# Two-token loads, ScalarE's first issues and an in-flight cast of half of w_out, in a fused RWKV attention and feed-forward kernel

## The chip, the cores and the metric

The kernel runs on 1 core of one Trainium2 chip. The metric is the device time of one execution in microseconds (us), the median of several runs. TensorE is PE in the profile (PEld is its weight load), VectorE is DVE, ScalarE is ACT, GpSimd is POOL, and SyncE, which issues most of the DMAs, is SP.

## The reference, cut to what matters

```python
# r, k, v: (4, 8, 768, 48) f32 (batch, head, token, dim); w, u: (8, 48); w_in: (384, 2048); w_out: (2048, 384)
for t in range(S):
    cur = np.einsum('bhd,bhe->bhde', u[None] * kt, vt)
    y[:, :, t] = np.einsum('bhd,bhde->bhe', rt, state + cur)
    state = w[None, :, :, None] * state + np.einsum('bhd,bhe->bhde', kt, vt)
x = y.transpose(0, 2, 1, 3).reshape(B * S, H * D)          # 3072 tokens x 384
h = x @ w_in
g = np.where(h >= 1, h, np.where(h <= -1, 0.0, (h + 1) ** 2 / 4))
out = g @ w_out
```

## The kernel before, in words

**Units.** The 4 x 768 tokens are cut into 24 units of 128 tokens (C = 128; unit i is batch i mod 4, chunk i div 4). Two units make a block m of 256 tokens (UB = 2, 12 blocks). The kernel has no loop at run time on its main path: everything is unrolled, and the data stay on the core between the stages.

**Attention of a unit** (`attention`, L469). K, R and V of the unit are loaded as 128 tokens by 8 heads by 48 (`add_load`, L417: tiles K, R, Vf; each row that the DMA moves is 48 floats, 192 bytes). K times `Winv` (w to the power -j-1, op "kw", L483) and R times `Wpow` (w to the power i, "rw", L487) go to one bf16 tile KR; PE or a DMA transposes it to RK ("tr" L505 and "rk", or "trd" L524). "at" (L535) forms K times R for all token pairs in two PSUM tiles, "mask" (L550, L553) keeps the lower triangle on DVE; "P", "dg", "dc" (L565, L571, L579) get the diagonal term with u on PE for units below `dmm`, and two GpSimd multiplications with a DVE sum (L585, L586, L591) for the others. "vd" (L596) multiplies the diagonal by V, "y" (L606, L609) is the product with V and with the carried state, "x" (L621) adds the two. "xp" and "xt" (L631) transpose x on PE for units below `xpe`; the others use a DMA transpose (L639). "x2" (L647) sums the squares of x for a bound. "st", "t", "tw", "bd" (L657, L664, L668, L672) carry the state. The first four units have no earlier state.

**The feed-forward** takes xT. `layer1` (L697): per block eight groups "L1" of six matmuls (L715) of 128 by 128 weights with 256 tokens, each group squared by ACT into g (L730; (h/2 + 1/2) squared, and a check at the end repeats the work in full only where some |h| could exceed 0.95). `layer2` (L735): per unit four groups "L2" of four matmuls (L749) with 384 columns, group s using quarter s of w_out; then a copy of the output tile and its store.

**The weights** w_in and w_out come in four quarters each, I0 to I3 and O0 to O3 (L443 to L462): a f32 load of 768 KB into a staging tile wf (5 slots), and three or four casts to bf16 by whichever of ACT, DVE and POOL the planner picks (profile line L318, the helper `copy`).

**The order.** `Plan.run` (L98) is a list scheduler run at build time. Each operation has a table of engines with costs, a due time (CFG "due", "step" and "bias"), buffers and dependences; it writes out one fixed order for each engine, and each engine then runs its list strictly in that order. The order of the first loads on SP comes from CFG "order": U0 to U3 (the loads of units 0 to 3), I0 to I3, O0, O1, O2, U4, U5, O3, U6, U7. All loads and stores are issued by SP, but for one small load of u by ACT (L379). Each DMA issued by SP or ACT takes one of eight completion semaphores in turn, so each one waits for the one eight before it.

**Fillers.** Until a planned time PE runs matmuls on a zero tile wherever it would otherwise be idle (L403, "wm"). They are placed in the fixed order too.

**Start.** w is loaded, spread to 128 partitions by two matmuls (L367), its logarithm lw is taken by ACT (L373), then `Winv` and `Wpow` by two exponentials (L375, L376).

Of the kernel before, what the change touches and what calls it, by code (L numbers as in the profile page):

```python
# [16 lines left out]
CFG = {  # L17
    "order": "U0 U1 U2 U3 I0 I1 I2 I3 O0 O1 O2 U4 U5 O3 U6 U7",
    "tpe": 10,
    "dmm": 8,  # L20
    "xpe": 6,
    "pair": 4,
    "cold": 9.0,
    "fine": 0,
    "am0": 2,
    "am1": 0,
    "norm": 100.0,
    "wide": 0,
    "due": [32.65, 38.55, 28.55, 31.54, 45.68],
    "step": 9.83,  # L30
    "warm": 24.0,
# [3 lines left out]
    "bias": {  # L35
        "P": 2.76, "am": -14.26, "at": -12.0, "bd": -7.97, "cI": 4.41, "cO": 11.29, "c_uw": 4.37, "dc": 5.73,
        "dg": 7.99, "ku": -5.64, "kw": 7.93, "ldK": -0.11, "ldR": 0.75, "ldVf": 1.96, "mask": -7.09, "red": 3.59,
        "rk": -1.31, "rkk": 0.04, "rkr": 5.61, "rw": -4.62, "st": 7.95, "t": -0.44, "tr": 0.61, "trd": -2.94,
        "trk": -6.22, "trr": 1.71, "tw": -8.79, "v": 0.76, "vd": -0.65, "x": 1.06, "x2": 1.39, "xp": -2.11,
        "xt": 0.98, "xtd": -1.36, "y": -5.96,  # L40
    },
# [20 lines left out]
class Plan:  # L62
# [35 lines left out]
    def run(self):  # L98
# [13 lines left out]
        while len(done) < len(todo):  # L112
# [47 lines left out]
            if e == "DVE" and o.sb and free["POOL"] > est + 0.15:  # L160
                occ, lat = occ + free["POOL"] - est - 0.15, lat + free["POOL"] - est - 0.15
            if e == "PE" and est < CFG["cold"] and o.name[:2] != "wm":
                occ, lat = 2.0 * occ, lat + occ
# [55 lines left out]
def kernel(  # L219
# [30 lines left out]
    while len(D_m) < NB + 2:  # L250
# [10 lines left out]
        "K": 6, "R": 6, "Vf": 6, "wf": 5, "KR": 4, "KU": 3, "V": 6, "RK": 4, "AT": 3, "P": 2, "VD": 3, "dg": 3,  # L261
        "x": 5, "x2": 2, "g": 5, "os": 3, "sq": 1, "ss": 2, "am": 2,
    }
    P = Plan(slots)
    rows = rot.tile([1, 2, H, DP], F32, name="rows", tag=f"g_{slots['g'] - 1}")
    lw = rot.tile([128, H, D], F32, name="lw", tag="x2_1")

    def get(b, shape, dtype):
        pl = psum if b.pool in ("a", "h", "o") else rot
        nm = f"{b.pool}_{b.slot}"  # L270
        b.t = pl.tile(shape, dtype, name=nm, tag=nm)
        return b.t
# [3 lines left out]

    nc.scalar.preload_act_table_set("natural_log_exp_and_others")

# [14 lines left out]
    i_col = const.tile([128, 1], F32, name="i_col")  # L293
    negj_col = const.tile([128, 1], F32, name="negj_col")
    Wpow = const.tile([128, H, D], F32, name="Wpow")
    Winv = const.tile([128, H, D], F32, name="Winv")
# [23 lines left out]
    def pair(t, p):  # L320
        return t[:, 2 * p : 2 * p + 2, :].rearrange("q h d -> q (h d)")
# [5 lines left out]
    heads = lambda t: t.rearrange("p (h d) -> p h d", h=H)  # L327
    c_wr = P.op("c_wr", {"SP": (0.5, 0)}, lambda e: nc.sync.dma_start(out=w_sp[0:128:64, :], in_=w.rearrange("(s h) d -> s (h d)", s=2)), due=-1000, dma=(0.05, 1, 0.5))
    c_ubc = P.op("c_ubc", {"SP": (0.4, 0)}, lambda e: nc.sync.dma_start(out=u_bc, in_=row_bcast(u)), due=D_m[CFG["dmm"] // UB] - 25, dma=(0.7, 8, 0.6))
    c_cols = P.op("c_col", {"POOL": (0.2, 0.2)}, lambda e: nc.gpsimd.iota(i_int, pattern=[[0, 1]], base=0, channel_multiplier=1), due=-100)  # L330

    def f_kr(i):
        def fn(e):
            nc.vector.memset(KR[i], 0.0)
        return fn

    kr0 = [P.op(f"c_kr{i}", {"DVE": (0.48, 0.5)}, f_kr(i), due=-90 + i) for i in range(slots["KR"])]

    def f_col(e):
        nc.vector.tensor_copy(i_col, i_int)  # L340
        nc.vector.tensor_scalar(negj_col, i_col, -1.0, -1.0, ALU.mult, ALU.add)
    c_icol = P.op("c_icol", {"DVE": (0.3, 0.35)}, f_col, deps=[c_cols], due=-92)
    c_ident = P.op("c_ident", {"POOL": (0.6, 0.7)}, lambda e: make_identity(nc, ident), due=-98)
# [9 lines left out]
    c_um = P.op("c_um", {"POOL": (0.8, 0.8)}, f_um, due=-97)  # L353

    def f_z(e):
        nc.vector.memset(zero, 0.0)  # L356
        nc.vector.memset(onesf, 1.0)
        nc.vector.memset(ones, 1.0)
        nc.vector.memset(uw, 0.0)
# [4 lines left out]
    def f_wb(e):  # L364
        for s in range(2):
            get(wbb[s], [128, H // 2, D], F32)
            mm(wbb[s].t, onesf[s * DP : s * DP + 1, :], w_sp[s * DP : s * DP + 1, :], start=True, stop=True)  # L367
    c_wb = P.op("c_wb", {"PE": (0.27, 0.35)}, f_wb, deps=[c_wr, c_z], allocs=wbb, due=-98)
    lws = [slice(s * H // 2, (s + 1) * H // 2) for s in range(2)]

    def f_lw(e):
        for s in range(2):
            nc.scalar.activation(lw[:, lws[s]], wbb[s].t, AF.Ln)  # L373
    c_lw = P.op("c_lw", {"ACT": (0.58, 0.65)}, f_lw, deps=[c_wb], uses=wbb, due=-98)
    c_winv = P.op("c_winv", {"ACT": (0.5, 0.58)}, lambda e: nc.scalar.activation(Winv, lw, AF.Exp, scale=negj_col), deps=[c_lw, c_icol], due=-97)  # L375
    c_wpow = P.op("c_wpow", {"ACT": (0.5, 0.58)}, lambda e: nc.scalar.activation(Wpow, lw, AF.Exp, scale=i_col), deps=[c_lw, c_icol], due=-96)  # L376
    c_lrow = P.op("c_lrow", act(384, False), lambda e: nc.scalar.copy(rows[:, 0, :, 0:D], lw[0:1]), deps=[c_lw, c_rz], due=8.2)
# [21 lines left out]
    for i in range(160):  # L399
        def f_wm(e, i=i):  # L400
            if wmb.t is None:
                get(wmb, [128, 256], F32)
            mm(wmb.t, zero[:, 0:128], zero, start=True, stop=True, skip_group_check=True)  # L403
        wm0 = P.op(f"wm{i}", {"PE": (0.22, 0.39)}, f_wm, deps=[c_z], uses=[wmb] if i else [], allocs=[] if i else [wmb], after=[wm0] if i else [], due=2000.0, late=CFG["warm"] if i else None)
    def f_tz(b):
# [8 lines left out]

    loads = {}

    def add_load(i):  # L417
        b, c = units[i]
        t0 = c * C
        res = {}  # L420
        due = LD[i]
        for j, (nm, src) in enumerate((("K", k), ("R", r), ("Vf", v))):
            bf = Buf(nm)

            def fn(e, bf=bf, src=src):
                t = get(bf, [128, H, D], F32)
                nc.sync.dma_start(out=t, in_=src[b, :, t0 : t0 + C, :].rearrange("h s d -> s h d"))  # L427

            o = P.op(f"ld{nm}{i}", {"SP": (0.5, 0)}, fn, after=[loads[i - 1][nm][1] if i else None], allocs=[bf], due=due + 0.1 * j, dma=(1.08, 64, 0.6))
            res[nm] = (bf, o)  # L430
        loads[i] = res

    LD = {}
    ORDER = CFG["order"].split()
    pos = {s: i for i, s in enumerate(ORDER)}
    for i in range(NU):
        LD[i] = -200.0 + pos[f"U{i}"] if f"U{i}" in pos else D_m[i // UB] - 18 + 2 * (i % UB)
# [4 lines left out]
    w_in_ready, w_out_ready = {}, {}  # L442
    for tag, q in [(x[0], int(x[1:])) for x in ORDER if x[0] in "IO"]:  # L443
        bf = Buf("wf")
        if tag == "I":
            src, dst, shape = w_in_src[:, :, q * FQ : (q + 1) * FQ], w_in_sb[:, :, q * FQ : (q + 1) * FQ], [128, nKb, FQ]
        else:
            src, dst, shape = w_out_src[:, q * TQ : (q + 1) * TQ, :], w_out_sb[:, q * TQ : (q + 1) * TQ, :], [128, TQ, d_out]
        nd = 24 if tag == "I" else 32
        res = w_in_ready if tag == "I" else w_out_ready  # L450
        due = -200.0 + pos[f"{tag}{q}"]
        def fn(e, bf=bf, src=src, shape=shape):
            t = get(bf, shape, F32)
            nc.sync.dma_start(out=t, in_=src)  # L454
        o = P.op(f"ld{tag}{q}", {"SP": (0.6, 0)}, fn, allocs=[bf], due=due, dma=(2.05, nd, 0.6))
        res[q] = []
# [12 lines left out]
    def attention(i):  # L469
# [6 lines left out]
        (Kb, Ko), (Rb, Ro), (Vb, Vo) = loads[i]["K"], loads[i]["R"], loads[i]["Vf"]  # L476
        krb, vb, rkb, atb, yb, xb = Buf("KR"), Buf("V"), Buf("RK"), Buf("AT"), Buf(A), Buf("x")
        both = {**pool(384), "DVE": (0.51, 0.56)}
        prev = state.get(b)

        def f_kw(e):
            krb.t = KR[krb.slot]
            V_ENG[e].tensor_mul(krb.t[:, H:, 0:D], Kb.t, Winv)  # L483
        o_kw = P.op(f"kw{i}", both, f_kw, deps=[Ko, c_winv] + kr0, uses=[Kb], allocs=[krb], due=D0 - 6)

        def f_rw(e):
            V_ENG[e].tensor_mul(krb.t[:, :H, 0:D], Rb.t, Wpow)  # L487
        o_rw = P.op(f"rw{i}", both if soft else {"DVE": both["DVE"]}, f_rw, deps=[Ro, c_wpow, o_kw], uses=[Rb, krb], due=D0 - 5.8)

# [4 lines left out]

        if by_pe:
            trb = Buf(A)
# [153 lines left out]
        if c < NCH - 1:  # L650
            stb = Buf(A)
            DS = D_m[m + 2] + 1.5 * j

            def f_st(e):
                get(stb, [128, NP, 2 * D], F32)
                for p in range(NP):
                    mm(stb.t[:, p, :], pair(krb.t[:, H:, :], p), pair(vb.t, p), start=True, stop=True)  # L657
            o_st = P.op(f"st{i}", pe(0.17), f_st, deps=[o_kw, o_v], uses=[krb, vb], allocs=[stb], due=D0 - 0.2 if c else DS - 10)

# [112 lines left out]

    n_dma = sum(1 for o in P.ops if o.dma is not None) + NU + 1
    TWICE = range(12, 12 + -n_dma % 8)
# [122 lines left out]
```

## Time and profile before

| what | value |
|---|---|
| time, median of 14 runs | 180.8 us (178.54 to 182.68) |
| the profiled execution | 179.31 us, its span 177.5 us |
| mean granted PE clock | 0.993 |
| PE busy | 167.0 us (94%), 1719 matmuls |
| ACT busy | 121.3 us (68%) |
| DVE busy | 111.6 us (63%) |
| POOL busy | 99.7 us (56%) |
| L1 (L715), 576 matmuls | 77.0 us busy |
| L2 (L749), 400 matmuls | 76.0 us busy |
| fillers (L403), 47 matmuls | 10.4 us busy |
| moved by DMA | 31.14 MB in 104,717 packets |
| K, R, Vf loads | 192 KB each, 4.2 us from issue to landing (median) |

The span runs from the first instruction to the last; the rest of the execution lies around it. Matmuls are pipelined, so that the busy time of a short group holds a tail that the next group overlaps; the time from the start of one group to the start of the next says what a group really takes of PE.

### The profile page before, as it was taken

The numbers are of one execution on the slowest core, as the hardware profiler recorded it, in microseconds if no ns is written. First come the engines' busy times: TensorE is split into PE (matmuls) and PEld (weight loads), VectorE is DVE, ScalarE is ACT, GpSimd is POOL, SyncE is SP. The second block draws the span as 40 slices with busy tenths as digits, with TensorE's granted clock in tenths as the row PEclk, the third lists the DMA queues.
The fourth block names the chain that finished last, engine by engine and source line by source line (L and its number), as shares of the span: only waits on it lengthen the run. The fifth ranks groups of instructions, "written<-read, shape, count | busy, mean of one in ns | idle before, by whom it ended". The sixth has DMA issues, their size and how long they took to land.

```text
span 177.5 us, 4529 instructions
## 1 busy us (share of the span) xinstructions
PE 167.0 (94%) x1719; PEld 126.3 (71%) x1719; DVE 111.6 (63%) x220; ACT 121.3 (68%) x267; POOL 99.7 (56%) x138
## 2 busy tenths in 40 slices
PE   7999888979999999999999899999999999999990
PEld 4776676767678777777777677777777867777770
DVE  5599995589897986768753795797674818010000
ACT  4656777786769689468855596894896955755620
POOL 8235273127697879938495389599797940300000
PEclk9999999999999999999999999999999999999997
DMA  4999999799997989999498997997988863311111
GB/s 80 192 192 338 345 377 317 142 277 178 210 202 162 206 183 171 161 195 220 95 208 167 211 212 150 180 216 148 207 162 189 174 131 94 89 52 44 46 44 50
DMA packets 104717, 31.14 MB, mean 175 GB/s; under 512 B 97778, under 2 KB 103156, under 8 KB 104692
## 3 DMA queue, kind: packets, MB, share of 16 engines
q1 hardware_dynamic: 104676, 30.81, 80.2%
q8 instruction: 14, 0.23, 0.6%
q14 instruction: 11, 0.09, 0.2%
q10 hardware_dynamic: 16, 0.00, 0.0%
HBM read 20.65 MB, written 4.72 MB: 143 GB/s over the span
## 4 chain that ended last, share of the span: by engine, by line
PE 64%; DMA 14%; SPq 12%; POOL 4%; DVE 1%; issue 1%; ACT 0%; POOLq 0%
PE o L749 30%; PE h L715 25%; SPq L427 9%; DMA wf<-in_moe_w_in_dram 6%; DMA wf<-in_moe_w_out_dram 3%; DMA Vf<-in_v_dram 2%; PE a L535 2%; PE a L609 2%; DMA R<-in_r_dram 2%; PE a L606 2%; SPq L454 1%; PE a L657 1%; DMA xTa<-x 1%; PE a L505 1%; POOL T L668 1%
## 5 line engine op out<-in xcount | busy, mean ns | idle before, releaser
L715 PE MATMUL h<-xTa,w_in_sb 128*128 128x256 bf16 x576 | 77.0, 273 | 0.7 <-ACT w_in_sb L318 0.6
L749 PE MATMUL o<-w_out_sb,g 128*128 128x384 bf16 (+2 forms) x400 | 76.0, 319 | 0.7 <-DVE w_out_sb L318 0.6
L730 ACT ACTIVATE g<-h 128x512 bf16<-128x512 f32 x96 | 56.6, 595 | 27.6 <-PE h L715 26.4
L715 PEld LDWEIGHTS <-w_in_sb 128*128 128x128 bf16 x576 | 54.5, 98 | 14.2 <-ACT w_in_sb L318 1.1
L749 PEld LDWEIGHTS <-g 128*128 128x128 bf16 x400 | 36.9, 98 | 16.3 <-issue 0.9
L553 DVE TENSOR_TENSOR AT<-a,umask 128x512 bf16<-128x512 f32 x46 | 28.9, 683 | 8.5 <-PE a L535 8.4
L596 POOL TENSOR_TENSOR VD<-V,dg 128x384 f32<-128x384 bf16 x18 | 15.5, 865 | 12.4 <-ACT V L318 7.5
L586 POOL TENSOR_TENSOR KU<-KU,R 128x384 f32<-128x384 f32 x16 | 17.9, 1116 | 6.4 <-DMA R<-in_r_dram 5.4
L487 DVE TENSOR_TENSOR KR<-R,Wpow 128x384 bf16<-128x384 f32 x22 | 15.4, 698 | 6.1 <-DMA R<-in_r_dram 5.9
L585 POOL TENSOR_TENSOR KU<-K,u_bc 128x384 f32<-128x384 f32 x16 | 18.3, 1143 | 0.0
L318 ACT CAST Tbd<-T 48x192 bf16<-48x192 f32 x38 | 13.3, 349 | 5.3 <-POOL T L668 4.1
L621 DVE TENSOR_TENSOR x<-a,VD 128x384 bf16<-128x384 f32 x24 | 13.0, 552 | 5.4 <-PE a L609 5.1
L483 DVE TENSOR_TENSOR KR<-K,Winv 128x384 bf16<-128x384 f32 x16 | 12.3, 776 | 2.5 <-ACT Winv L375 1.6
L647 ACT ACTIVATE x<-x 128x384 bf16<-128x384 bf16 x24 | 12.5, 520 | 1.2 <-DVE x L621 0.7
L318 ACT CAST V<-Vf 128x384 bf16<-128x384 f32 x20 | 10.2, 508 | 4.2 <-DMA Vf<-in_v_dram 4.1
L318 ACT COPY os<-o 128x384 f32<-128x384 f32 (+2 forms) x21 | 9.7, 463 | 4.5 <-PE o L749 3.9
L668 POOL TENSOR_TENSOR T<-T,wc 128x192 f32<-128x192 f32 x20 | 10.8, 548 | 3.0 <-ACT T L318 2.5
L591 DVE TENSOR_REDUCE dg<-KU 128x8 f32<-128x384 f32 x16 | 8.8, 547 | 5.0 <-POOL KU L586 4.8
L664 DVE TENSOR_TENSOR T<-T,a 48x192 f32<-48x192 f32 x32 | 11.2, 349 | 1.1 <-PE a L657 0.4
L403 PE MATMUL o<-zero 128*128 128x256 bf16 x47 | 10.4, 355 | 1.1 <-DVE zero L356 1.1
L800 POOL TENSOR_TENSOR ss<-sq 128x256 bf16<-128x256 bf16 x8 | 6.3, 787 | 8.3 <-ACT sq L791 8.3
L483 POOL TENSOR_TENSOR KR<-K,Winv 128x384 bf16<-128x384 f32 x8 | 8.3, 1040 | 3.0 <-DMA K<-in_k_dram 2.1
(83 smaller groups left out, 168.0 us busy)
## 6 DMA issues: line engine op xcount, KB each, us to landing
K<-in_k_dram SPq DMA_DIRECT2D x24, 192.0 KB, 4.2
R<-in_r_dram SPq DMA_DIRECT2D x24, 192.0 KB, 4.2
Vf<-in_v_dram SPq DMA_DIRECT2D x24, 192.0 KB, 4.2
out_dram<-os SPq DMA_DIRECT2D x19, 192.0 KB, 3.2
wf<-in_moe_w_in_dram SPq DMA_DIRECT2D x4, 768.0 KB, 8.7
wf<-in_moe_w_out_dram SPq DMA_DIRECT2D x4, 768.0 KB, 10.3
out_dram<-os SPq DMA_DIRECT2D x8, 96.0 KB, 2.2
xTa<-x SPq DMA_TRANSPOSE x18, 2.6
```

Of the source, the lines that this page charges most:

```text
L318: (nc.scalar.copy if eng == "ACT" else V_ENG[eng].tensor_copy)(o, i)
L427: nc.sync.dma_start(out=t, in_=src[b, :, t0 : t0 + C, :].rearrange("h s d -> s h d"))
L483: V_ENG[e].tensor_mul(krb.t[:, H:, 0:D], Kb.t, Winv)
L487: V_ENG[e].tensor_mul(krb.t[:, :H, 0:D], Rb.t, Wpow)
L553: nc.vector.tensor_mul(atb.t[s], at_p[s].t, umask4)
L585: nc.gpsimd.tensor_mul(kub.t, Kb.t, u3)
L586: nc.gpsimd.tensor_mul(kub.t, kub.t, Rb.t)
L596: V_ENG[e].tensor_mul(vdb.t, vb.t, dgb.t[:, :, None].to_broadcast([128, H, D]))
L621: nc.vector.tensor_add(xb.t, yb.t[:, 0:384].rearrange("p (h d) -> p h d", h=H), vdb.t)
L715: mm(hb.t[:, f, :], w_in_sb[:, kk, c * 128 : (c + 1) * 128], xT[m][:, kk, cols], start=(kk == 0), stop=(kk == nKb - 1))
L730: nc.scalar.activation(gb[m].t[:, 2 * n : 2 * n + 2, :], hb.t, AF.Square, bias=0.5, scale=0.5)
L749: mm(ob.t[:, : hi - lo], gb[m].t[:, f, j * C : (j + 1) * C], w_out_sb[:, f, lo:hi], start=(f == 0), stop=(f == nN - 1))
```

## The change

The change rewrites the start of the kernel and the tables that steer the planner.

- **Two-token loads** ("duo": 2, units 0 to 3). K and R of two units share one staging tile of 128 partitions. One DMA per unit and tensor puts two neighbouring tokens (96 floats, 384 bytes) on one partition; unit 0 has the even partitions, unit 1 the odd ones. The multiplications are then made for even and odd tokens of both units (z = 0, 1), with four tables W2 of powers (2i, 2i+1 and their negatives) in place of Winv and Wpow, which are made later for the other units. Four transposes of four matmuls each fill two PSUM tiles, and the copies to RK (two per unit, on ACT or DVE) pick the unit's columns with a stride of two. Because KR no longer holds the tokens of a unit in order, units 0 to 3 transpose their K back on PE ("kb", four matmuls) and copy it ("kc") for the state.
- **ScalarE issues** the loads of K and R of unit 0; the table load of ACT becomes an operation behind them.
- **O2 and O3 by GpSimd**: a DMA on POOL's own queue reads f32 and writes bf16 straight into w_out_sb: no staging tile and no casts. O2 waits for O0 to land, O3 for O1.
- **Order of the weights**: O0 U4 O1 U5 O2 O3 in place of O0 O1 O2 U4 U5 O3.
- **Tables**: "fine": 2 makes the L1 groups of blocks 0 and 1 work on one unit (12 matmuls of 128 tokens in place of 6 of 256), so that they wait for one unit's x alone; dmm 8 to 6 (units 6 and 7 take the GpSimd path of the diagonal); xpe 6 to 10 (units 6 to 9 transpose x on PE); pair 4 to 3 (block 3's "at" as one group); am0 2 to 1; new due times and biases. The fillers' cost in the plan is halved, so there are 74 of them.

```diff
-    "order": "U0 U1 U2 U3 I0 I1 I2 I3 O0 O1 O2 U4 U5 O3 U6 U7",
+    "order": "U0 U1 U2 U3 I0 I1 I2 I3 O0 U4 O1 U5 O2 O3 U6 U7",
-    "dmm": 8,
-    "xpe": 6,
-    "pair": 4,
-    "cold": 9.0,
-    "fine": 0,
-    "am0": 2,
+    "dmm": 6,
+    "xpe": 10,
+    "pair": 3,
+    "cold": 6.5,
+    "duo": 2,
+    "sw": "O2 O3",
+    "fine": 2,
+    "am0": 1,
...
+    for q in range(4):
...
+            nc.scalar.activation(W2[:, q], lw, AF.Exp, scale=i2_col[:, q : q + 1])
...
+                            (nc.scalar if e == "ACT" else nc.sync).dma_start(out=bf.t[x:128:2, j], in_=src[b, :, t0 : t0 + C, :].rearrange("h (i s) d -> i h (s d)", s=2))
...
+                f"ls{x}", {"POOL": (0.85, 0.85)}, lambda e, src=src, dst=dst: nc.gpsimd.dma_start(out=dst, in_=src),
+                deps=wld[-2:-1], after=[before], due=due, dma=(2.15, 2, 1.4),
...
+                        src = dd["D"].t[:, q].rearrange("p h (s d) -> p h s d", s=2)[:, :, z]
+                        V_ENG[e].tensor_mul(kb.t[:, H - q * H : 2 * H - q * H, 0:D], src, W2[:, 2 * q + z])
...
+                            nc.tensor.transpose(tb.t[:, z, p, :], pair(dd["kr"][z].t, NP - q * NP + p), ident)
...
+                dst = rkb.t[:, NP - q * NP : 2 * NP - q * NP, :].rearrange("a p (i s) -> a s p i", s=2)
+                copy(e, dst, dd["tr"][q].t[:, :, :, j:128:2])
...
+                    for p in range(NP):
+                        nc.tensor.transpose(kbp.t[:, p, :], rkb.t[:, NP + p, :], ident)
```

## The prediction, made before the changed kernel had run

> **What bounds the kernel now.** First the page: the 40 slices, then the first line of the chain that ended last.
>
> ```profile
> PE   7999888979999999999999899999999999999990
> DMA  4999999799997989999498997997988863311111
> GB/s 80 192 192 338 345 377 317 142 277 178 210 202 162 206 183 171 161 195 220 95 208 167 211 212 150 180 216 148 207 162 189 174 131 94 89 52 44 46 44 50
> PE 64%; DMA 14%; SPq 12%; POOL 4%; DVE 1%; issue 1%; ACT 0%; POOLq 0%
> ```
>
> A slice is 4.44 us. PE looks full from the second slice on, but part of that is fillers. Slices 2 and 3 move 192 GB/s (the 192-byte rows of K, R and V), slices 5 and 6 345 and 377 (weights). The chain in order of time:
>
> ```profile
> 13.90 9.84 DMA wf<-in_moe_w_in_dram
> ...
> 33.17 5.35 DMA wf<-in_moe_w_out_dram
> 38.58 1.09 POOL w_out_sb L318 x2
> 39.71 0.81 PE o L749 x4
> ```
>
> Up to 39.71 loads set the pace; from there the chain is nearly all PE. So three questions: when the first L1 group starts, what PE loses between it and the group that needs O3, and whether the work after it changes. The timeline of the engines, and then two stretches of the table by windows (columns: PE, PEld, DVE, ACT, POOL busy, clock, DMA share, GB/s):
>
> ```profile
> 13.91 0.51 ACT L318 CAST V<-Vf 128x384 bf16<-128x384 f32 x1
> ...
> 15.96 1.01 DVE L621 TENSOR_TENSOR x<-a,VD 128x384 bf16<-128x384 f32 x2
> ...
> 18.98 0.83 PE L715 MATMUL h<-xTa,w_in_sb 128*128 128x256 bf16 x6 [0.20 <-ACT w_in_sb L318]
> ...
> 20.35 0.82 PE L715 MATMUL h<-xTa,w_in_sb 128*128 128x256 bf16 x6
> ...
> 21.01 0.36 PE L609 MATMUL a<-V,AT 128*128 128x48 bf16 x8
> ...
> 21.21 0.24 PE L571 MATMUL a<-uw,P 128*128 128x2 bf16 x4
> ...
> 39.27 0.40 PE L535 MATMUL a<-RK 48*128 48x128 bf16 x8 [1.03 <-ACT RK L318]
> ```
>
> ```profile
> 20.00:30.00 10.00, 8.59 (x100) 6.75 (x100) 7.65 (x18) 7.57 (x15) 5.29 (x9) 1.00 1.08 360
> 30.00:40.00 10.00, 8.68 (x92) 6.76 (x90) 7.20 (x16) 8.19 (x18) 2.48 (x4) 1.00 0.93 218
> ```
>
> Unit 1's V is cast only at 13.91, and both x of block 0 follow at 15.96. From start to start, an L1 group takes 0.66 (20.35 to 21.01) and y 0.20 (21.01 to 21.21). In the same way at takes 0.33 (37.21 to 37.54), st 0.17 (23.29 to 23.46), dg 0.10 (40.73 to 40.83), the state part of y 0.17 (40.36 to 40.53), xp 0.17 (25.93 to 26.10), tr 0.45 (35.36 to 35.81), L2 0.65 (34.71 to 35.36).
>
> **PE's account before.** From 18.98 to 39.71 PE did 16 L1 (10.56), 3 L2 (1.95), st of units 2 and 3 (0.34), at of 3, 4 and 5 (0.99), dg of 2 to 4 (0.30), y (0.40) and xp (0.34) of 2 and 3, tr of 4 and 5 (0.90): 15.8 us. So it lost 4.95 of 20.73: 2.74 idle (0.20, 0.39 for w_in casts, 0.39, 0.22 for w_out casts, 0.51 for x, 1.03 for RK), about 1.0 fillers, the rest ends of groups.
>
> **The change, part by part.**
>
> *Loads.* A unit's load of 196,608 bytes takes 1.02 us at 192 GB/s; a weight quarter of 786,432 bytes 2.10 at 375. Twelve unit loads and I0 to I3 are 20.7 us of DMA, and I3's cast started at 23.87. A 192-byte row costs one of 16 DMA engines 16 ns (64 rows in 1.02 us), a 2-KB row of w_in 87 ns (24 in 2.10). I have no row of 384 bytes: on the straight line between these two it costs 23 ns, so a load takes 0.75 us. Bounds: 0.52 (the weights' rate) and 1.02 (no gain). Eight such loads save 2.2 us (0 to 4.0), so I3 lands near 21.7; R4 (1.0) and O0 (2.1) follow by 24.8, against a cast at 27.9. V of units 0 and 1 now stands ahead of K and R of 2 and 3: behind four two-token loads and w: 5.0 us of DMA, landed near 8, not 13.9.
>
> *Start of ScalarE.* It issues K0 and R0, waits for the small load of w (used at 2.68), issues the load of u (1.25, its row), then loads its table (1.28): lw at 5.2, against 3.93. If the issue costs 0.69, as w's own does, lw is at 4.7. Then lw 0.55 and four tables W2 at 0.53 (Winv to Wpow, start to start): the fourth product, for which all later steps wait, starts at 7.9. Before, the first started at 5.16.
>
> *Unit 0 to its x.* Product to 8.5; in PE's list the transposes of the u rows stand ahead of the last transposes of R (0.93, to 9.4), then those (0.4) and their copy (0.42 to 0.69; with stride two, taken at 0.55). In PE's list ten fillers stand ahead of the first at: at 0.11 to 0.23 each (rows at 17.20 and 3.63), the mask can begin near 11.8. Then DVE's own list: masks 0.68 and 0.65, copy 0.42, uw 0.34, product 0.56, copy 0.55, VD 0.54, copy 0.55, masks 1.30, x 0.50, cast 0.43, x of unit 1 0.50, copy of xT 0.35: 7.4 us. **First L1 near 19.2**, against 18.98. The earlier V gains nothing, because DVE is late instead.
>
> *From the first L1 to the group that needs O3.* PE's new list holds 16 L1 (12 matmuls of 128 columns: eight transposes of that size take 0.61 with a tail of 0.17, so 0.055 each and 0.66 a group, no loss), 3 L2, at and st of units 2 to 5, dg of 2 to 4, y and xp of 2 to 4, tr of 4 and 5: 17.0 us. That is 0.33 (at of unit 2) that lay before, and 0.88 (st of 4 and 5, y and xp of 4) that came after 39.71. So the new list is equal with the old one at 39.71 + 0.88 = 40.6. Without loss PE gets there at 19.2 + 17.0 = 36.2: a gain of 4.4 less the new loss. From the 4.95 I take the weight waits (1.2; I1 to I3 and O0 land 2 to 3 us earlier), 0.6 of fillers (four are left), 0.5 (x of unit 2 is now covered by L1 groups of block 0) and half of the 1.03 (tr of unit 5 stands farther ahead of its at): **loss 2.0**. Cover that is not free: ACT. From its first cast at 16.0 to the 14th squaring, which frees the PSUM tile of the last L1, its rows sum to 17.8 (14 g at 0.54, five casts at 0.57, four x2 at 0.51, T and Tbd pairs at 0.64 and 0.72, others 2.6): 33.8 with no wait. PE wants it at 35.3. Idle 4.2 us, as in these two stretches before, ACT would cost PE 2.7.
>
> *O2 and O3 on GpSimd.* No staging, no casts (before: 38.58 to 39.71 behind the landing). O1 lands by 31.0 (24.8, K4, V4, O1 and O2), O3 between 34 and 37.2; it is wanted at 38.2. At the slow rows' rate (4.1 us for a quarter) it costs 1.1. GpSimd has no row for issuing a DMA: bounds are SP's 0.43 and 3.80 (a weight quarter at 22.48); I take 1.0, near the unhindered 0.69 and 1.25. It then costs nothing: GpSimd is through with O0's casts at 26.8 (DVE, by 5.4 us more of its list, copies unit 3's diagonal at 24.6; VD 0.83, two casts 1.40), then issue, V cast 0.5, issue, two casts of O1: 28.7 + 2 issues = 30.7 (O1's landing makes it 33); PE wants O1 at 32.6, so up to 0.4 is in the 2.0.
>
> *Later.* Units 6 to 9 add xp (0.68), units 6 and 7 drop dg (0.20): +0.5 on a full PE. GpSimd gets 2 x 2.3 us more at 56% busy, ACT or DVE four copies of 0.35 to 0.47, SP loses four transposes: covered. In both lists 14 L1 groups and 23 or 24 L2 groups stand behind the last y, so the end is alike.
>
> **Sum:** 4.4 - 2.0 - 0.5 = 1.9 us. The profiled execution took 179.31 (span 177.5 and 1.8 around it) and would take 177.4. It is 1.5 below the median of 180.8, so the median goes to **178.9**.
>
> One rule speaks against this. In 19 to 40 DVE runs casts from SBUF to SBUF (seven of w_out alone, 492 ns each). The Trainium skill, "SBUF — State Buffer", section "SBUF: two separate sides", says that while VectorE runs a two-port copy GpSimd cannot write descriptors, and that a GpSimd DMA of 0.62 us took 3.1 beside one. No row here shows it. By that figure, as an estimate, GpSimd's line ends at 34.9 and the sum is 181.2.
>
> **Rivals.**
>
> 1. *Larger gain.* ACT's issue is short (-0.55), PE's fillers run at 0.11 (-1.1): first L1 at 17.5, loss 1.0. 40.6 - 17.5 - 17.0 - 1.0 - 0.5 = 4.6: **176.2**. For it: V no longer waits. Against: the first 17 fillers took 0.23 to 0.24 each (1.46 us for six, 2.53 for eleven).
> 2. *Hidden.* Only the weight waits go: loss 3.75, gain 4.4 - 3.75 - 0.5 = 0.15: **180.6**. For it: DVE and ACT are near full in both stretches. That the two-token rows move no faster (I3 at 23.9 again, wanted by the fourth L1 near 22.3) ends here too.
> 3. *Slower: GpSimd is held by its two issues.* Casts of O1 stand behind the second one. From 1.95 us an issue each further microsecond costs PE two; from 2.9 the gain is gone, from 3.4 it is a loss of over 0.9. At 3.80: 28.7 + 7.6 = 36.3, a wait of 3.7, **182.6**. For it: the V cast and the casts of O1 stand in that line, and a DVE op at 13.26 was stretched from 0.54 to 1.24 beside a GpSimd op. Against: GpSimd is 25% busy from 30 to 40.
>
> **How the numbers follow.** Forecast 0.37, larger gain 0.15, hidden 0.22, slower 0.26. About 0.5% (0.9 us) is what a measurement can tell from no change: faster 0.52, same 0.22, slower 0.26. The range reaches toward both outer cases, with a tenth left out on each side: 175.8 to 182.6. The forecast's own range is 177.6 to 179.9.
>
> **What would show it.** Right: first L1 at 18.5 to 20, I3's cast near 22, PE without fillers and full by 38, an issue on GpSimd near 1.0. Wrong: a first L1 off by over 1.5; a wait of L2 for GpSimd's casts of O1 or for O3; over 4 us lost between; a new PE gap past 41.

## The result, and the profile after

The changed kernel takes 183.55 us in the median (182.0 to 185.47), the kernel before 180.89 beside it (178.54 to 184.53): a ratio of 1.0172, 95% interval 1.0134 to 1.0209. (Ratios leave out executions that took over 1.5% more than the fastest of the same kernel.) It is slower, and above the range that was given. Its profiled execution took 183.4 us with a span of 181.5, against 179.31 and 177.5: 4.0 us more span; the profiled execution of before lay 1.6 below its median, so the medians differ by 2.7.

The 40 slices and the first line of the chain, of the changed kernel (a slice is 4.54 us):

```profile
PE   7599899999999999999999999999998999999990
DMA  4999999799687899898979879968979950311111
GB/s 106 219 225 327 380 265 237 132 190 188 178 175 162 186 192 205 173 192 176 159 160 173 184 167 176 206 127 156 196 178 157 212 127 0 87 47 45 45 43 49
PE 76%; DVE 6%; DMA 5%; POOL 5%; ACT 3%; issue 2%; ACTq 0%; POOLq 0%
```

The chain has less DMA in it (5% for 14%): loads no longer set the pace. But PE's second slice is at 5 where it was 9. The windows of 20 to 40 us (columns as before) show PE fuller than before, 9.12 and 9.82 for 8.59 and 8.68 (up to 24.67 a part of it is fillers):

```profile
20.00:30.00 10.00, 9.12 (x149) 7.87 (x149) 9.50 (x20) 9.19 (x24) 6.09 (x11) 1.00 1.00 273
30.00:40.00 10.00, 9.82 (x164) 8.97 (x165) 8.26 (x16) 9.14 (x22) 6.45 (x10) 1.00 1.02 182
```

So the stretch that the change was to fill is fuller, and the loss lies ahead of it. The timeline of the changed kernel from the start (start, length, engine and line):

```profile
0.75 0.75 ACTq L457 DMA_DIRECT2D wf<-in_k_dram  x1
1.53 0.92 ACTq L457 DMA_DIRECT2D wf<-in_r_dram  x1
4.40 1.23 ACTq L405 DMA_DIRECT2D rows<-in_u_dram  x1
5.66 1.28 ACT L334 ACT_TABLE_LOAD   x1 [5.66 <-POOL T L434]
6.95 0.55 ACT L385 ACTIVATE lw<-a 128x192 f32<-128x192 f32 x2
8.19 2.27 DVE L563 TENSOR_TENSOR KR<-wf,W 128x384 bf16<-128x384 f32 x4 [5.58 <-ACT W L391]
8.80 0.61 PE L576 MATMUL a<-ident,KR 128*128 128x128 bf16 x4 [2.02 <-DVE KR L563]
12.53 2.34 PE L429 MATMUL o<-zero 128*128 128x256 bf16 x10
14.80 0.61 PE L647 MATMUL a<-RK 48*128 48x128 bf16 x8
15.54 0.69 DVE L665 TENSOR_TENSOR AT<-a,umask 128x512 bf16<-128x512 f32 x1 [0.82 <-PE a L647]
24.67 0.83 PE L844 MATMUL h<-xTa,w_in_sb 128*128 128x128 bf16 x12
43.57 1.46 PE L878 MATMUL o<-w_out_sb,g 128*128 128x384 bf16 x8
```

The first L1 group starts at 24.67 (18.98 before, 19.2 forecast), the group that needs O3 at 43.57 (39.71). Between the second and the third issue of ScalarE lie 1.95 us in which nothing runs on it, and the table load and lw stand behind: lw at 6.95 for 3.93. The same two steps in the kernel before:

```profile
2.63 1.25 ACTq L379 DMA_DIRECT2D rows<-in_u_dram  x1
3.93 0.55 ACT L373 ACTIVATE lw<-a 128x192 f32<-128x192 f32 x2 [1.90 <-POOL T L408]
```

From 6.78 to 8.80 PE idles; after that its transposes (four in 0.61) and fillers (ten in 2.34) still run at the slow rate. (The first record of the granted clock in the trace, at full speed, begins at 17.35, and there four transposes fall to 0.39. Ahead of a first record the profile prints 1.00 all the same.)

### The profile page after: what moved, and what is told of

It reads as the page before. It is cut to its first block, busy times and chain, and to the rows that moved or that the text cites. A ratio compares the mean times of both kernels' runs of the same rounds, so it can differ in the third digit from the quotient of the medians.

```text
span 181.5 us, 4813 instructions
## 1 busy us (share of the span) xinstructions
PE 171.2 (94%) x1862; PEld 131.9 (73%) x1862; DVE 109.2 (60%) x219; ACT 121.7 (67%) x270; POOL 110.0 (61%) x151
## 4 chain that ended last, share of the span: by engine, by line
PE 76%; DVE 6%; DMA 5%; POOL 5%; ACT 3%; issue 2%; ACTq 0%; POOLq 0%
PE o L878 31%; PE h L844 29%; DMA RK<-KR 5%; PE a L647 3%; PE o L429 2%; PE a L721 2%; PE a L718 2%; PE a L786 2%; DVE AT L665 2%; PE a L617 1%; DVE w_in_sb L324 1%; PE a L576 1%; DVE x L733 1%; POOL Tbd L433 1%; DVE KR L563 1%
## 5 line engine op out<-in xcount | busy, mean ns | idle before, releaser
L844 PE MATMUL h<-xTa,w_in_sb 128*128 128x256 bf16 (+1 forms) x672 | 78.5, 257 | 0.5 <-ACT g L857 0.4
L878 PE MATMUL o<-w_out_sb,g 128*128 128x384 bf16 (+2 forms) x400 | 77.0, 320 | 0.0
L844 PEld LDWEIGHTS <-w_in_sb 128*128 128x128 bf16 x672 | 56.9, 98 | 12.7 <-issue 0.3
L708 POOL TENSOR_TENSOR VD<-V,dg 128x384 f32<-128x384 bf16 x20 | 17.0, 854 | 9.3 <-DVE dg L703 5.0
L698 POOL TENSOR_TENSOR KU<-KU,R 128x384 f32<-128x384 f32 x18 | 19.4, 1080 | 3.5 <-DMA R<-in_r_dram 2.3
L697 POOL TENSOR_TENSOR KU<-K,u_bc 128x384 f32<-128x384 f32 x18 | 20.1, 1118 | 0.0
L429 PE MATMUL o<-zero 128*128 128x256 bf16 x74 | 15.2, 352 | 1.1 <-DVE zero L366 1.1
L703 DVE TENSOR_REDUCE dg<-KU 128x8 f32<-128x384 f32 x18 | 9.8, 546 | 5.9 <-POOL KU L698 5.9
L929 POOL TENSOR_TENSOR ss<-sq 128x256 bf16<-128x256 bf16 x8 | 5.3, 668 | 10.1 <-ACT sq L920 9.9
L429 PEld LDWEIGHTS <-zero 128*128 128x128 bf16 x74 | 8.4, 124 | 3.6 <-DVE zero L366 1.1
```

Of the source, the lines that this page charges most:

```text
L697: nc.gpsimd.tensor_mul(kub.t, Kb.t, u3)
L698: nc.gpsimd.tensor_mul(kub.t, kub.t, Rb.t)
L708: V_ENG[e].tensor_mul(vdb.t, vb.t, dgb.t[:, :, None].to_broadcast([128, H, D]))
L844: mm(hb.t[:, f, :], w_in_sb[:, kk, c * 128 : (c + 1) * 128], xT[m][:, kk, cols], start=(kk == 0), stop=(kk == nKb - 1))
L878: mm(ob.t[:, : hi - lo], gb[m].t[:, f, j * C : (j + 1) * C], w_out_sb[:, f, lo:hi], start=(f == 0), stop=(f == nN - 1))
```

## The experiments

Three theories. **One**: the loss is ScalarE's start, where the issue of u's load is late. **Two**: fillers, at the slow rate, stand in PE's list ahead of "at" and "kb". **Three**, formed after the first runs: GpSimd's two transfers delay loads that wait in SP's queue. How long a load takes to land is counted from its issue ("V of unit 5 lands after 6.7 us"). Ratios are to the kernel before, timed on the same chip.

### u's issue and the fillers

`w_first`: w's load put at the head of the order in which operations are written.

```diff
+    done.remove(c_wr)
+    done.insert(0, c_wr)
```

> The changed kernel with one thing moved: w's small load is the first DMA in the program's order, K of unit 0 the second; every engine's own list stays as it was. The load of u is the ninth DMA, so it takes the completion semaphore of the first one, and in the changed kernel that first one is K of unit 0 (192 KB) instead of w (1.5 KB). Theory 1 (ScalarE's start: u's issue waited at 4.40 for K0's landing and held the table load and lw at 6.95): u's issue now follows w's landing near 2.65, lw near 5.2, the fourth product starts near 8.2 instead of 9.9; the first L1 group moves from 24.7 to about 23, the time from 183.5 to about 182. Theory 2 (cold fillers standing in PE's list ahead of at and kb): lw moves too, but the first L1 stays within 0.5 of 24.7 only if PE's or VectorE's list, not lw, sets the chain; time 183 to 184.

Ratio 1.0158 (1.0075 to 1.024), first L1 at 24.48. The edit did not reach the built program, where ScalarE's first DMA stayed first and all lists and semaphores as they were: it is a second measurement of the changed kernel, and says nothing on the theories.

`u_late`: u's load issued behind the four tables.

```diff
+    done.remove(c_ur)
+    done.insert(done.index(c_w2[3]) + 1, c_ur)
```

> The changed kernel with u's load issued by ScalarE behind the four tables W2 instead of ahead of the table load. Theory 1: the table load starts near 2.5, lw near 4.5 (it still needs PE's spread of w, at 3.52 behind eleven fillers), the W2 tables near 5.1, all products and PE transposes about 2.4 earlier; first L1 near 22.3, time near 181.2. Theory 2: lw comes early but ten fillers, at, kb and six fillers keep their place, and the loads of K and R of units 0 and 1 (landing near 6) now set the first product; the first L1 gains under 1.

Ratio 1.016 (1.0061 to 1.0258), span 180.1 for 181.5. In its timeline the table load follows the issue of R at once, and the first L1 comes 3.75 us sooner:

```profile
2.47 1.28 ACT L334 ACT_TABLE_LOAD   x1 [2.47 <-issue]
4.57 0.55 ACT L385 ACTIVATE lw<-a 128x192 f32<-128x192 f32 x2 [0.81 <-PE a L379]
9.37 0.40 PE L576 MATMUL a<-ident,KR 128*128 128x128 bf16 x4
9.60 1.25 PE L429 MATMUL o<-zero 128*128 128x256 bf16 x10
20.92 0.83 PE L844 MATMUL h<-xTa,w_in_sb 128*128 128x128 bf16 x12
28.14 2.87 SPq L473 DMA_DIRECT2D Vf<-in_v_dram  x1
28.56 0.93 POOL L513 DMA_DIRECT2D w_out_sb<-in_moe_w_out_dram  x1
38.66 0.50 POOL L324 CAST V<-Vf 128x384 bf16<-128x384 f32 x1 [4.00 <-DMA Vf<-in_v_dram]
39.22 0.33 PE L786 MATMUL a<-V,KR 128*128 128x96 bf16 x4 [2.48 <-POOL V L324]
```

More than the 2.4 of the wait, since PE now runs at the fast rate from 7.74 on: ten fillers take 1.25 for 2.34, four transposes 0.40 for 0.61. Theory one holds for the first L1. But the time hardly follows: V of unit 5, issued at 28.14, is there only at 38.66, and PE stands 2.48 us for it. That wait is not in the changed kernel, and no theory had it.

`few_fillers`: only the first 24 of 74 fillers.

```diff
+    late = [o for o in done if o.name[:2] == "wm"][24:]
+    done = [o for o in done if o not in late]
```

> The changed kernel with only the first 24 of its 74 filler matmuls (the two lists of eleven and ten, and three more); from the ten fillers ahead of the first at on there is none. No result depends on them. Theory 2: at comes at about 13.6 instead of 14.8 and kb's copy no longer waits (1.0), so the first L1 moves by 1.3 to 2.2, to 22.5 to 23.4, and the time to about 182. Its price, if PE keeps its slow start for longer without fillers: transposes at 0.61 instead of 0.39 past 17.4, up to 1 us back. Theory 1: PE waits for ScalarE's and VectorE's chain anyway and the first L1 moves by less than 0.7; time 183 to 184.

Ratio 1.0053 (1.001 to 1.0095): 1.2% better than the changed kernel. "at" starts at 13.39, the first L1 at 22.68: 2.0 sooner, though the group runs at the slow rate (1.44 us). With the late start of the changed kernel, theory two holds too.

`u_late_few_fillers`: both edits.

> Both edits: u's load behind the four tables W2, and only the first 24 fillers. If the two causes add: first L1 near 24.7 - 2.4 - 1.7 = 20.6, time near 179.5 to 180, no slower than the kernel before. If a third limit lies under them (the two-token scheme's own longer chain on VectorE and ScalarE), the first L1 stays above 22 and the time above 181.

Ratio 1.0027 (0.9982 to 1.0072), the first L1 at 20.90, as with u late alone: the two do not add. In `u_late`, where PE is fast, the fillers cost the first L1 nothing. Here PE is slow again (the granted clock is 0.50 from 12 to 24), and that costs the first L1 nothing either, as no filler is left to run at that rate: u's wait is worth 3.75 with all fillers and 1.8 with 24. The time is under that of `u_late` all the same, and PE does not wait for V of unit 5:

```profile
28.89 2.00 SPq L473 DMA_DIRECT2D Vf<-in_v_dram  x1
35.66 0.49 POOL L324 CAST V<-Vf 128x384 bf16<-128x384 f32 x1
```

It is there 6.8 us behind its issue, though GpSimd issues its two transfers at 29.05 and 30.45. This counts against theory three in its simple form.

### GpSimd's transfers

`kr0_by_sp`: K and R of unit 0 issued by SP.

```diff
+        if o.name in ("ldK0", "ldR0"):
+            o.eng = "SP"
```

> The changed kernel with K and R of unit 0 issued by SP behind w instead of by ScalarE; all else in the same order. Theory 1 (ScalarE's start): u's issue no longer takes the completion semaphore of a 192 KB load and starts near 1.9, the table load near 3.2, lw at 4.5, right behind PE's spread of w; the first product near 5.8, the first L1 group within 0.5 of the 20.9 that it had with u's load issued late, unless R of unit 1, issued fifth on SP, lands after 7 and holds the R products (then 21 to 22). Rival: the early K and R are worth what the part was meant to bring; without them the first product waits for K past 7 and the first L1 stays above 23. Time 181 to 182.5 by theory 1, 183.5 by the rival.

u's issue starts at 1.89, lw at 4.57, the first L1 at 20.62, as early as in any run of the changed kernel: theory one again. Yet the ratio is 1.0303 (1.0175 to 1.043). The timeline of GpSimd:

```profile
28.40 0.94 POOL L513 DMA_DIRECT2D w_out_sb<-in_moe_w_out_dram  x1
29.79 0.75 POOL L513 DMA_DIRECT2D w_out_sb<-in_moe_w_out_dram  x1
39.11 0.50 POOL L324 CAST V<-Vf 128x384 bf16<-128x384 f32 x1 [4.59 <-DMA Vf<-in_v_dram]
```

V of unit 5 (issued 28.60) is late again, beside GpSimd's issues. PE waits 2.04 for it, and then its clock falls: from 39 to 45 the granted clock is 0.50 and an L1 group takes 1.44, so that the group that needs O3 starts only at 45.49.

`no_gpsimd_dma`: O2 and O3 through SP and casts, all placed anew by the planner.

```diff
-    "sw": "O2 O3",
+    "sw": "",
```

> The changed kernel with O2 and O3 loaded by SP into staging tiles and cast, as before; the planner places them anew, so other orders move too. If GpSimd's DMAs are neutral or help: first L1 within 0.5 of 24.7, the group that needs O3 up to 1.5 later (casts of 1.1 behind the landing, and four transfers behind each other), time 183.5 to 185. If they do harm (one V load took 10.5 us to land beside them when u's load came late): no load of K, R or V above 8 us between 25 and 45, time 181.5 to 183.

Ratio 1.0262 (1.0134 to 1.039), the group that needs O3 at 44.68: 1.1 later. So the GpSimd part seems to help the changed kernel; its ratio of 1.0172 lies within this interval, and other orders moved too, so it is not shown.

`before_gpsimd_dma`: the kernel before with this part alone, placed anew.

```diff
+        if tag == "O" and q >= 2:
+            o = P.op(
+                f"ls{tag}{q}", {"POOL": (0.85, 0.85)}, lambda e, src=src, dst=dst: nc.gpsimd.dma_start(out=dst, in_=src),
+                deps=wld[-2:-1], due=due, dma=(2.15, 2, 1.4),
+            )
+            res[q] = [o]
+            wld.append(o)
+            continue
...
```

> The kernel before with this one part of the change: O2 and O3 cast in flight by GpSimd's queue, O2 behind O0's landing, O3 behind O1's. If the part helps by itself: the casts of 1.1 us behind O3's landing go from the chain, the group that needs O3 starts 0.5 to 1.5 earlier than 39.71, time 0.5 to 1.3 under the kernel before. If it is hidden: within 0.5. If it harms, by holding GpSimd's casts of O0 and O1 or by slowing the loads of K, R and V beside it: 1 to 2 us more than before.

Ratio 1.0517 (1.0404 to 1.0629; its five times spread from 184.94 to 189.74). The chain of this run in order of time:

```profile
25.89 10.38 DMA K<-in_k_dram
36.29 0.56 DVE KR L492
36.85 0.61 DVE RK L318
37.51 0.61 PE a L544 x8
```

K of unit 5, 10.38 us behind its issue, with GpSimd's issues at 25.91 and 28.09; PE waits 2.90 for it. That wait is a part of the loss only: the group that needs O3 starts at 41.24, 1.5 later than in the kernel before.

`u_late_gap_fillers`: u late, and only the ten and the six fillers ahead of "at" and "kb" left out.

```diff
+    late = [o for o in done if o.name[:2] == "wm"][24:40]
+    done = [o for o in done if o not in late]
```

> u's load issued late, and of the fillers only the ten ahead of the first at and the six ahead of the second kb left out; the other 58 stay. Leaving out all but 24 saved as much as theory 2 said, but its first L1 groups ran at 1.44 instead of 0.83 us. If the sixteen are only in the way: first L1 at 19.5 to 20.3 (0.6 to 1.4 under the 20.9 with u late), L1 groups at 0.83, time 180.5 to 181.5. If they are covered by ScalarE's and VectorE's chain once PE is warm (1.25 and 0.82 us then instead of 2.34 and 1.49): first L1 at 20.6 to 21.2, no change against u late.

First L1 at 22.24, later than with u late alone. Its four times spread from 179.75 to 185.29 (ratio 1.0219, 1.0077 to 1.0361), so the ratio settles little here.

`u_late_gq_late`: u late, and GpSimd's two issues behind its casts of O1.

```diff
+    late = [o for o in done if o.name in ("lsO2", "lsO3")]
+    done = [o for o in done if o not in late]
+    at = max(n for n, o in enumerate(done) if o.name[:3] == "cO1" and o.eng == "POOL") + 1
+    done[at:at] = late
```

> u's load late (first L1 at 20.9 in that run, but only about 1.3 us of 3.75 kept), and GpSimd's issues of O2 and O3 moved behind its two casts of O1 (31.4 to 32.4) instead of 28.6 and 30.0. Theory 3 (GpSimd's two transfers run beside SP's queue and delay the loads of unit 5 that are already queued: V of unit 5, issued at 28.1, landed 10.5 us later, about two transfers of 2.1 us more than its place in SP's queue explains, and PE stood 2.5 us for it): V lands by 35.5 to 37, PE's wait near 37 shrinks to under 0.7, span 177.5 to 178.5, time 179.5 to 180.5. Rival: V is late by SP's own queue (768 KB of O1 ahead of it): it lands after 38 all the same, O2 and O3 come later on top, time 182.5 or more.

Ratio 1.0056 (1.0012 to 1.01). GpSimd's timeline:

```profile
31.88 1.68 POOL L513 DMA_DIRECT2D w_out_sb<-in_moe_w_out_dram  x2
34.53 0.50 POOL L324 CAST V<-Vf 128x384 bf16<-128x384 f32 x1
```

V of unit 5 (issued 27.82) is there by 34.53, within 6.7 us for 10.5: 3.8 less, nearly the two transfers of 2.1. PE no longer waits for it; it waits 0.70 for O3 instead and reaches that group at 40.55 for 42.45. For this plan, where nothing else was moved, theory three is shown. The Trainium skill, "DMA: Bandwidth & Descriptors", section "Queues, rings and completion order", says that each DMA engine takes turns between the queues that have work for it. That agrees: a transfer on a second queue does not line up behind the loads of the first, it takes its turns among them. What decides how much a load loses stays open: with one GpSimd transfer ahead of it V of unit 5 took 8.8 us in `one_token`, with two issued just behind it 10.5 in `u_late` and 6.8 in `u_late_few_fillers`.

`before_gq_late`: the same four lines in `before_gpsimd_dma`.

> The kernel before with O2 and O3 by GpSimd's queue, but issued behind GpSimd's cast of O1 (near 30.7) instead of at 25.9 and 28.1. Theory 3: K of unit 5, issued at 25.9 and landed 10.4 us later in the first version, lands by 32.5, PE's wait of 2.9 for its RK goes, and the time falls from 188 by 3 to 5 us, to 183 to 185; what is left is O2 and O3 arriving late for L2 (40 and 42). Rival (the issues hold GpSimd itself, or casts in flight are slow as such): 187 or more.

K of unit 5 lands after 6.1 us, the group that needs O3 starts at 39.14 for 41.24 (39.71 in the kernel before). But the ratio stays at 1.0438 (1.0362 to 1.0515): 187.16 us, the time that the rival gave. The rest of the loss comes far later. The windows from 100 to 140 us of this run:

```profile
100.00:120.00 20.00, 16.13 (x177) 11.79 (x175) 14.59 (x28) 14.34 (x35) 14.08 (x17) 0.95 0.94 178
120.00:140.00 20.00, 20.00 (x165) 14.17 (x163) 9.96 (x16) 13.29 (x28) 15.75 (x21) 0.88 0.89 175
```

The kernel before has PE at 19.50 and 20.00 there with the clock at 1.00. From 100 to 120 ScalarE waits 3.0 us for loads of V (and PE 3.0 for it), GpSimd 2.1 for K, VectorE 2.6 for R, and the granted clock then falls to 0.88. The planner had placed all later loads anew; whether that or the GpSimd queue is to blame was not separated.

`kr0_by_sp_gq_late`: the edits of `kr0_by_sp` and of GpSimd's late issues together.

> K and R of unit 0 issued by SP, and GpSimd's issues of O2 and O3 behind its casts of O1. If the 185.5 of the first version was the collision of its early start with GpSimd's transfers: V of unit 5 lands 1.5 to 3 us sooner after its issue than 10.5, PE's wait near 38 shrinks from 2.0 to under 0.8, time 180 to 181.5, as with u's load late. If ScalarE's issues are worth something by themselves: 182.5 or more.

180.62 us, where `kr0_by_sp` took 185.47 on another chip; V of unit 5 takes 6.7 us, the clock stays at 1.00, and the group that needs O3 starts at 40.03 for 45.49. The collision was the cause of that loss. The ratio is 1.0161 (1.0071 to 1.0251) of a kernel before that ran at 178.63 there; whether ScalarE's two issues are worth anything stays open, the first L1 (20.63, against 20.80 in `u_late_gq_late`) says no.

### What is left

`best_try`: the edits of `u_late`, of `few_fillers` and of GpSimd's late issues together.

> u's load late, only the first 24 fillers, and GpSimd's issues of O2 and O3 behind its casts of O1. If the three causes add (3.75 of the first L1, the wait for V of unit 5, fillers in front of at and kb): first L1 at 20.5 to 21, the group that needs O3 at 40 to 41, time 178.5 to 179.8, up to 1% under the kernel before. If the cold L1 groups (1.44 us) that follow without fillers take back what the fillers cost, 180 to 181 and no difference from the kernel before.

Ratio 1.0055 (1.0015 to 1.0094), no better than with all fillers, with the first L1 at 20.78.

`gap_gq_late`: the edits of `u_late_gap_fillers` and of GpSimd's late issues together.

> u's load late, GpSimd's issues behind its casts of O1, and the sixteen fillers ahead of the first at and the second kb left out, the other 58 kept. If the sixteen stand in the way: first L1 at 19.6 to 20.4 and time 179 to 180. If PE, once warm, runs them in the shadow of ScalarE and VectorE (1.25 and 0.82 us): first L1 within 0.3 of 20.8, time 180 to 180.8. If leaving them out lets PE go back to its slow rate (the first run of this kind had first L1 at 22.2): first L1 at 21.5 to 22.5, time 180.5 to 182.

Ratio 1.0112 (1.0057 to 1.0168), first L1 at 21.81: 1.0 later than with them. Four transposes at 13.28 take 0.59 again (0.38 with the fillers): PE has gone back to its slow rate (the granted clock is 0.50 from 12 to 18), and the fillers that are left now run at it. In `best_try`, slow there too but with none left, the first L1 came at 20.78.

`gap_gq_late_wb`: in addition five of the eleven fillers ahead of w's spread.

```diff
-    late = [o for o in done if o.name[:2] == "wm"][24:40]
+    wm = [o for o in done if o.name[:2] == "wm"]
+    late = wm[6:11] + wm[24:40]
```

> As gap_gq_late, and five of the eleven fillers ahead of PE's spread of w left out. If the spread waits for the fillers and lw for it: the spread at 2.6 instead of 3.5, lw near 3.8 (the table load ends at 3.75) instead of 4.57, the K products 0.7 sooner, the R products held by their loads near 6.5; first L1 0.2 to 0.7 sooner than in gap_gq_late, if PE warms as early. If PE's idle time then delays its warming: first L1 0.5 to 2 later.

lw starts at 3.78 for 4.57, but four transposes take 0.61 still at 9.60 (0.40 at 9.17 in `gap_gq_late`), and the first L1 (21.64) gains 0.17; ratio 1.0139 (1.0082 to 1.0195). The early fillers are not what holds it.

`one_token`: the two-token loads undone, with the load order of the kernel before, placed anew.

```diff
-    "duo": 2,
+    "duo": 0,
...
-        "ldK": -8.4, "ldR": 1.53, "ldVf": 1.51,
+        "ldK": -0.11, "ldR": 0.75, "ldVf": 1.96,
```

> The changed kernel with the loads of units 0 to 3 one token a row again, in the order of the kernel before, and so without ScalarE's two issues, the four tables W2 and the kb and kc steps; the planner places all anew from the changed tables (88 fillers). If the two-token scheme is the loss (longer chain on VectorE, ScalarE and PE): first L1 at 19 to 21, time 179.5 to 181.5. If the tables (due times, fillers, orders) and the GpSimd queue are the loss whatever the loads: first L1 as late or later than 22 or a wait for loads of units 4 and 5 past 30, time 183 or more.

Ratio 1.0142 (1.0053 to 1.023), first L1 at 22.57: `u_late` is 1.7 better there, with another order of everything. Its first L1 is as the second expectation had it, its time lies between the two.

No version beat the kernel before, and the 0.3 to 0.6% that the best of them lose were not traced.

## Why the prediction was wrong

By the terms of its sum, from the two profiled executions (us):

| term | predicted | measured | off by |
|---|---|---|---|
| first L1 group | 19.2 | 24.67 | -5.5 |
| from there to the group that needs O3: 17.0 and a loss of 2.0 | 19.0 | 18.90 | +0.1 |
| later, on a full PE | 0.5 | 1.0 | -0.5 |
| sum | gain of 1.9 | loss of 4.0 in span | -5.9 |

"Later" is what remains behind that group: 181.5 - 43.57 = 137.9, against 177.5 - 39.71 - 0.88 = 136.9.

**Start of ScalarE** is the step that failed. It had the load of u wait for w, "used at 2.68", as before. But a DMA takes one of eight completion semaphores in turn and waits for the one eight places before it. u's load is the ninth that takes one. Before, the semaphore it took was w's (1.5 KB, landed by 2.63); now it is that of K of unit 0 (192 KB), whose issue ScalarE was given: in the trace both carry number 100, K's last completion comes at 4.32, and u's issue follows at 4.40. In `kr0_by_sp`, where u's load has a semaphore of its own, it issues at 1.89. The fourth product started at 9.9 instead of 7.9: 2.0 of the 5.5. The rule stood in the description of the kernel; I never counted places in the new order.

**Unit 0 to its x** lost the other 3.5. PE waited for the products from 6.78 to 8.80 and was at the slow rate until 17.35; I took fillers at 0.11 to 0.23 and the mask at 11.8, and it came at 15.54 (1.7 beyond the 2.0). VectorE's list to the first L1 took 9.1 for 7.4: 1.03 of it is the wait for kb behind six fillers of 1.49 us, 0.50 a wait for ScalarE's copies of RK; VD took 0.77 for 0.54 and VectorE's copies of RK 0.73 for 0.55. `u_late` removes 3.75 of the 5.5 with one move.

**The loss of 2.0** and the 17.0 of work held to 0.1 us, and PE waited for no weight. That is in part the late start: I3 landed at 24.20, not 21.7, and nothing needed it before 24.67. But `u_late`, whose first L1 comes at 20.92, has no such wait either, and without the 2.48 for V its loss is 2.05. (My own terms come to 2.1, not 2.0.)

**O2 and O3 on GpSimd** "costs nothing" was right on its own terms (issues 0.94 and 0.75 us for the 1.0 taken, no wait for them), and the third rival is refuted: GpSimd was not held. The rule of the SBUF page that spoke against the change does not show in the issues either: they took 0.75 to 0.98 us in all runs, the one at 32.32 (0.94) beside two casts of w_out on VectorE (31.98 to 33.41). But the step asked only what the issues cost GpSimd, not what the transfers cost the loads beside them. In the changed kernel the late start put the issues at 32.32 and 33.71, behind V of unit 5. With the start as forecast they would have come near 28.7, and some 2.5 us of the gain could have gone there, as in `u_late`, or nothing, as in `u_late_few_fillers`. So the forecast of 178.9 could have failed at a second place.

**Loads**: from 3 to 6 us the changed kernel moves 276 GB/s for 207, a two-token load in 0.71 us (0.75 estimated), with two engines issuing; with SP alone (`kr0_by_sp`) it is 229 GB/s. But the weights are issued from 10.65 for 10.51: SP's issues follow one another without a break from 4.47, one of them for 2.32 us. In `u_late` I3 landed at 24.03, not 21.7. It bound nothing here, since the rest was late.

**Larger gain** and **hidden** supposed a first L1 at 17.5, or near the forecast's; neither came about.

## What to carry to other kernels

When a change moves a DMA in the order of issue, count the places of all completion semaphores again: a small load can inherit the semaphore of a large one, and whatever stands behind it on its engine waits too. A transfer that is moved to another queue is not only an issue on another engine: it can overtake what waits in the first queue, so ask which load lands last beside it, also for the case that the steps ahead get faster. An early wait can cost more than its length: here what stood behind it, fillers above all, ran at PE's slow rate (3.75 us lost with all fillers, 1.8 with 24).

## What the runs showed of the hardware

- PE started at 1.06 in every run and ran at half rate (four transposes 0.61, then 0.39) until the trace's first record of full clock: at 17.35 in the changed kernel, with a pause of 2.02 us at 6.78, at 7.74 in `u_late` without it. In the other runs with that pause it came at 17.55 to 17.59, and in six without it at 7.6 to 8.5. But the pause is not all: `best_try`, with no idle time of PE over 0.12 us up to 10.18, got it only at 16.47, `one_token`, with none up to its first L1, at 12.70. What decides it stays open. The Trainium skill, "TensorE: Matmul & The Clock Gate", section "Part 1: The HAM clock gate", puts the warm-up at some 3.4 us; no run here was as fast.
- After a wait of 2.04 us the clock fell to 0.50 for 6.8 us in `kr0_by_sp` (38.84 to 45.66); after one of 2.48 at the same place in `u_late` it did not.
- A load of 192 KB that was queued on SP landed 3.8 us later (10.5 for 6.7) in `u_late` and `kr0_by_sp`, where two GpSimd transfers of 768 KB each were issued just beside it, but not in `u_late_few_fillers` (6.8). GpSimd's transfers landed 5.4 to 9.1 us behind their issue.
